# GpSimd operations that carry a dependency on the latest two-operand step of VectorE

## The chip, the cores and the metric

The kernel runs on one core of a Trainium2 chip, as one launch. The metric is the device time of that launch in microseconds (us). Before the change it is 1239.37 us, the median of three runs (1239.02 to 1239.99). The engines are named as in the profile: PE is TensorE's matrix multiply and PEld its weight load, DVE is VectorE, ACT is ScalarE, POOL is GpSimd, SP is SyncE, which issues most of the transfers.

## The reference

The reference is attention over the 32 largest scores of each row, followed by a layer of three products of which the largest is taken, and an output product:

```python
scores = scale * np.matmul(q, k.transpose(0, 1, 3, 2))      # 8 batches, 8 heads, 576 x 576, head dim 64
kth = np.partition(scores, -32, axis=-1)[..., -32:-31]
scores = np.where(scores >= kth, scores, -1e9)
attn = softmax(scores)                                       # sum + 1e-9 in the denominator
x = (attn @ v) as (4608, 512)
h = np.maximum(np.maximum(x @ w1, x @ w2), x @ w3)           # 512 -> 768
out = h @ w_out                                              # 768 -> 512, float32
```

The weights are drawn as float64 numbers, so they reach the chip as pairs of 32-bit words.

## The kernel before

The attention is cut into units. A unit is one or two blocks of 128 query rows for a pair of heads (or the last 64 rows of two pairs), and it has two or four tiles of 128 rows by 576 scores. For each unit TensorE makes the scores (line 465), ScalarE copies them out of the accumulators into tiles `ssb` (473), and VectorE takes the eight largest of each of seven stretches of a row (482). From these small lists a pivot per row is worked out (lines 496 to 514); the last but one of its steps, line 512, is a scalar_tensor_tensor on two SBUF operands. ScalarE writes the sign of pivot minus score into a tile `w` and counts it (522). GpSimd multiplies score and sign, in place in `w` (line 527, the "window product"), VectorE takes the eight largest of the product (531, the MAX8 that follows a window product), and three small steps pick the threshold out of them (542, 545, 547). Then VectorE masks the scores in place (line 570: a scalar_tensor_tensor with two SBUF operands of 576 columns), ScalarE takes the exponential (579), TensorE transposes it (630) and multiplies it with the values (655), and the result is cut into a high and a low half of 16 bits: high by ScalarE (675), low by GpSimd (679).

The weights have to be turned from pairs of words into float32 first. This is the decode: three VectorE steps on 1024 or 512 columns (lines 257, 258, 259), of which the second and the third read two SBUF operands. ScalarE squares each decoded part (268), a scale follows from it (275, 285), ScalarE scales and casts the part (319, 322), and GpSimd subtracts for the low half (325). The scaled part lies in one of two buffers `ws` until GpSimd is done. The MLP's first layer (711) makes three products per block; ScalarE and VectorE take the largest (718, 720); ScalarE makes the high half (723) and GpSimd the low half (726). The second layer is line 771.

So GpSimd has five kinds of work: 288 window products (527), the low halves of the weights (325), of x (679) and of h (726), and eight small additions of a check (612).

The order of all this is not that of the source. Every step is a `Piece` with an engine, an estimated cost, the pieces that it needs, the ring of buffers that it takes and a rank. `in_order` (line 67) goes through the pieces like a clock: it picks the piece that can start earliest by its own estimates, calls its `run`, which writes the instructions, and moves the engine's estimated free time. So the instructions of each engine stand in a fixed order, that in which `run` was called, and they wait for each other by semaphores only as their data requires. Pieces of the MLP go into a list `fill` that TensorE takes from when nothing of the attention is ready.

Some VectorE pieces carry `alone=True`: the decode, the pivot's step 4 (line 512), the first two steps of the pick (542, 545), the mask (570) and a check (607). For these the planner's estimate keeps VectorE and GpSimd apart:

```python
        if x.alone:
            t = max(t, free["POOL"] + LOCK_A)
        elif x.engine == "POOL":
            t = max(t, shut[0] + LOCK_B)
```

Here `shut[0]` is the estimated end of the latest such piece, LOCK_A is -144 ns and LOCK_B is -103 ns. This sets the order and the estimated times only; no instruction waits for it.

Of the kernel before, what the change touches and what calls it, by code (L numbers as in the profile page):

```python
# [14 lines left out]
ALU = mybir.AluOpType  # L15
# [8 lines left out]
NW = 9  # L24
SHRINK = 2.0 ** -61
# [38 lines left out]
        self.size, self.users = size, []  # L64


def in_order(pieces, fill):

    queues, fills = {e: [] for e in LATE}, {e: [] for e in LATE}
    for x in sorted(pieces, key=lambda x: x.rank):
        queues[x.engine].append(x)
    for x in fill:
        fills[x.engine].append(x)
    free = {e: 0.0 for e in LATE}
    mode, shut = [None], [0.0]

    def ready(x):
        t = free[x.engine]  # L80
        for y in x.needs:
            if y.start is None:
                return None
            t = max(t, y.seen(x.engine) + x.slack)
        ahead = {}
        for ring, releases in x.takes:
            k = len(ring.users) - ring.size + ahead.get(ring, 0)
            ahead[ring] = ahead.get(ring, 0) + 1
            for y in ring.users[k] if k >= 0 else ():
                if y.start is None:  # L90
                    return None
                t = max(t, y.seen(x.engine))
        if x.engine == "PE":
            t += SWITCH[mode[0], x.mode]
# [5 lines that stand above are left out]
        return t  # L100

    left = len(pieces) + len(fill)
    while left:
        best = None
        low = min((q[0].rank for q in queues.values() if q), default=0.0)
        for e in LATE:
            some = [x for x in queues[e][:WINDOW] if x.rank <= low + LEAD]
            some = some + fills[e][:1] if e == "PE" else fills[e][:1] + some
            could = [(t, x) for x in some if (t := ready(x)) is not None]
            if could:  # L110
                other = could.pop() if e == "PE" and fills[e][:1] == [could[-1][1]] else None
                if could:
                    first = min(t for t, _ in could) + PATIENCE[e]
                    same = [c for c in could if c[1].mode and c[0] <= first + STICK] if e == "PE" and mode[0] else []
                    t, x = same[0] if same else next(c for c in could if c[0] <= first)
                    wait = STICK if same else SWITCH[mode[0], x.mode] + AHEAD_OF_FILL
                if not could or other and other[0] < t - wait:
                    t, x = other
                if best is None or t < best[0]:
                    best = t, x  # L120
        assert best, [(e, len(q), len(fills[e])) for e, q in queues.items()]
        t, x = best
        (fills if fills[x.engine][:1] == [x] else queues)[x.engine].remove(x)
        x.start = t
        free[x.engine] = t + x.cost
        if x.engine == "PE":
            mode[0] = x.mode
        if x.alone:
            shut[0] = t + x.cost
        for ring, releases in x.takes:  # L130
            ring.users.append(releases)
        x.run()
        left -= 1


# [13 lines left out]
def kernel(ctx, tc, q, k, v, moe_w1, moe_w2, moe_w3, moe_w_out, out):  # L149
    nc = tc.nc  # L150
# [99 lines left out]
    def decode(j, part):  # L250

        at0, n = place(j)
        raw = raw_of[j].rearrange("p c (n t) -> p (c n) t", t=2) if j < 3 * NB else raw_of[j].rearrange("p (n t) -> p n t", t=2)
        m = n // DECODES if j < 3 * NB else n
        low, top = (raw[:, part * m:(part + 1) * m, t] for t in range(2))
        w = wall.bitcast(I32)[:, at0 + part * m:at0 + (part + 1) * m]
        nc.vector.tensor_scalar(w, top, 3, 0x3FFFFFFF, ALU.logical_shift_left, ALU.bitwise_and)
        nc.vector.scalar_tensor_tensor(w, low, 29, w, ALU.logical_shift_right, ALU.bitwise_or)
        nc.vector.scalar_tensor_tensor(w, top, -0x40000000, w, ALU.bitwise_and, ALU.bitwise_or)

    squares_of = {}

# [44 lines left out]
    def cut(j, part):  # L307

        at0, n = place(j)
        m = min(n, 2 * CUT)  # L310
        at0 += part * m
        w = wall[:, at0:at0 + m].rearrange("p (c n) -> p c n", n=CUT)
        hi, lo = (wall.bitcast(F16)[:, 2 * at0:2 * (at0 + m)].rearrange("p (c t n) -> p t c n", t=2, n=CUT)[:, t] for t in range(2))
        box = {}

        def scaled():
            down = scale_of[f"w{j}"][0] if j < 3 * NB else scale_of["rows"][:, (j - 3 * NB) * P // CUT:(j - 3 * NB) * P // CUT + 1]
            box["ws"] = io.tile([P, 2 * CUT], F32, name="ws", bufs=2).rearrange("p (c n) -> p c n", n=CUT)
            nc.scalar.activation(box["ws"], w, AF.Copy, scale=down)

        def high():
            nc.scalar.copy(hi, box["ws"])

        def low():
            nc.gpsimd.tensor_tensor(lo, box["ws"], hi, ALU.subtract)  # L325
        return scaled, high, low

    pieces, fill = [], []
# [161 lines left out]
    def pivot(n, piece):  # L490

        d = st[n]
        nt, L, nA = d["nt"], d["L"], d.get("nA")
        if piece == 1:
            for t in range(nt):
                nc.vector.max(b9s[n % 3][:, t, 1:9], L[:, t, :, 4:8])
        elif piece == 2:
            n8 = d["n8"] = sm.tile([P, 4, 2, 8], F32, name="n8", bufs=NSM)
            for t in range(nt):
                nc.vector.max(n8[:, t, 0], nA[:, t].rearrange("p g j -> p (g j)"))  # L500
            nb = d["nb"] = sm.tile([P, 4], F32, name="nb", bufs=3)
            nc.vector.tensor_reduce(nb[:, :nt], nA[:, :nt, :, 0], AX.X, ALU.min)
        elif piece == 3:
            nR = sm.tile([P, 4, 4 * G], F32, name="nR", bufs=1)
            for t in range(nt):
                nc.vector.match_replace(nR[:, t], d["n8"][:, t, 0], nA[:, t].rearrange("p g j -> p (g j)"), -BIG)  # L506
            for t in range(nt):
                nc.vector.max(d["n8"][:, t, 1], nR[:, t])
        elif piece == 4:
            z = d["z"] = sm.tile([P, 4, 9], F32, name="z", bufs=2)  # L510
            low = d["n8"].rearrange("p t a b -> p t (a b)")[:, :nt, 4 * G - 24:4 * G - 15]
            nc.vector.scalar_tensor_tensor(z[:, :nt], low, -SHRINK, b9s[n % 3][:, :nt], ALU.mult, ALU.min)
        else:
            nc.vector.tensor_reduce(d["Q"][:, :, 0:1], d["z"][:, :nt], AX.X, ALU.max)  # L514

# [8 lines left out]
    def window(n, t):  # L524

        d = st[n]
        nc.gpsimd.tensor_tensor(d["w"][t], d["ssb"][t], d["w"][t], ALU.mult)  # L527

    def below(n, t):
        d = st[n]  # L530
# [2 lines left out]
    def pick(n, step):  # L533


        d = st[n]
        nt = d["nt"]
        if step == 0:
            d["oh"] = sm.tile([P, 4, NW], F32, name="oh", bufs=2)
        best = d["oh"]  # L540
        if step == 0:
            nc.vector.scalar_tensor_tensor(best[:, :nt], spots.unsqueeze(1).to_broadcast((P, nt, NW)), 1.0,
                                           d["cnt"][:, :nt].unsqueeze(2).to_broadcast((P, nt, NW)), ALU.mult, ALU.is_gt)
        elif step == 1:
            nc.vector.tensor_tensor(best[:, :nt], best[:, :nt], d["Q"], ALU.mult)
        else:
            nc.vector.tensor_reduce(d["kth"], best[:, :nt], AX.X, ALU.max)

# [17 lines left out]
    def mask(n, t):  # L566

        d = st[n]
        ss = d["ssb"][t]
        nc.vector.scalar_tensor_tensor(ss, ss, d["kth"][:, t:t + 1], ss, ALU.is_lt, ALU.subtract,  # L570
                                       accum_out=d["lost"][:, t:t + 1])

    def expo(n, t):
# [83 lines left out]
    def x_at(n, t):  # L657
        b, hps, us = units[n]
        if us[0] < NU:
            return t[:, hps[0], us[0] * P:(us[-1] + 1) * P]  # L660
        return t[:, hps[0]:hps[0] + 2, MAIN:S]
# [14 lines left out]

    def low_x(n):
        xh, xl = x_of[units[n][0]]
        nc.gpsimd.tensor_tensor(x_at(n, xl), xs_of(n), x_at(n, xh), ALU.subtract)  # L679
        st.pop(n)  # L680

    H, so_of = [], {}
    WIDE = S - 2 * P
# [2 lines left out]
    def mlp(b, first, spans, tiles, alone, needs, rank):  # L686
# [36 lines left out]
            nc.scalar.copy(H[0][:, f, cs], box["h"][:, :w])  # L723

        def low_h(f, cs, w, box):
            nc.gpsimd.tensor_tensor(H[1][:, f, cs], box["h"][:, :w], H[0][:, f, cs], ALU.subtract)  # L726

        for c0, c1 in spans:
            w = c1 - c0
# [258 lines left out]
    for b in range(B):  # L988
# [4 lines left out]
            fill.extend(every)  # L993
        x_done[b].append(last)

    with tc.manual_schedule():
        in_order(pieces, fill)


    limits = const.tile([P, 2], F32, name="limits")  # L1000
# [95 lines left out]
```

## Time and profile before

| | |
|---|---|
| median of three runs | 1239.37 us |
| profiled execution | 1238.17 us |
| its span, first to last instruction | 1236.4 us |
| PE busy | 1142.7 us, 8817 instructions |
| DVE busy | 1120.1 us, 5413 instructions |
| ACT busy | 1032.7 us, 2692 instructions |
| POOL busy | 570.5 us, 503 instructions |

The profile is one execution of the program. "Busy" is the time in which an engine had at least one instruction running; an instruction that is held by something inside the engine still counts as busy, so a held instruction shows as a longer one and not as idle time. Semaphore instructions don't count as busy. In the rows, `out<-in` gives the program's tiles, then the shape, then how often.

### The profile page before, as it was taken

The numbers are of one execution on the slowest core, as the hardware profiler recorded it, in microseconds if no ns is written. First come the engines' busy times: TensorE is split into PE (matmuls) and PEld (weight loads), VectorE is DVE, ScalarE is ACT, GpSimd is POOL, SyncE is SP. The second block draws the span as 40 slices with busy tenths as digits, with TensorE's granted clock in tenths as the row PEclk, the third lists the DMA queues.
The fourth block names the chain that finished last, engine by engine and source line by source line (L and its number), as shares of the span: only waits on it lengthen the run. The fifth ranks groups of instructions, "written<-read, shape, count | busy, mean of one in ns | idle before, by whom it ended". The sixth has DMA issues, their size and how long they took to land.

```text
span 1236.4 us, 27297 instructions
## 1 busy us (share of the span) xinstructions
PE 1142.7 (92%) x8817; PEld 778.5 (63%) x8817; DVE 1120.1 (91%) x5413; ACT 1032.7 (84%) x2692; POOL 570.5 (46%) x503
## 2 busy tenths in 40 slices
PE   5357877999899999999999999999999999999998
PEld 2124653566586766766676667666676767766765
DVE  7999998999999999999899999999899999999311
ACT  6588887999989898998889998998889989888421
POOL 2453654545445445355354554454553544546111
PEclk7576986999899999999999999999999999999999
DMA  6241220202010202011110102020101100000000
GB/s 240 71 141 52 63 82 11 88 2 69 18 54 18 61 1 86 2 48 31 49 31 27 52 10 78 3 72 6 49 31 48 31 25 23 10 10 1 18 18 29
DMA packets 25750, 54.38 MB, mean 44 GB/s; under 512 B 2688, under 2 KB 2944, under 8 KB 25600
## 3 DMA queue, kind: packets, MB, share of 16 engines
q1 hardware_dynamic: 25296, 52.14, 12.9%
q8 instruction: 71, 1.16, 0.4%
q14 instruction: 79, 0.65, 0.2%
q10 hardware_dynamic: 304, 0.43, 0.1%
HBM read 43.12 MB, written 9.44 MB: 43 GB/s over the span
## 4 chain that ended last, share of the span: by engine, by line
PE 37%; DVE 23%; ACT 7%; POOL 2%; issue 2%; DVEq 0%; ACTq 0%
PE m L711 17%; DVE L L482 6%; DVE ssb L570 5%; PE m L771 5%; PE tr L655 5%; PE s L465 4%; PE tr L630 4%; DVE Q L531 4%; ACT pm L579 2%; POOL w L527 2%; DVE h L720 2%; ACT w L522 1%; ACT pT L638 1%; DVE nR L506 1%; PE tr L627 1%
## 5 line engine op out<-in xcount | busy, mean ns | idle before, releaser
L527 POOL TENSOR_TENSOR w<-ssb,w 128x576 f32<-128x576 f32 x288 | 410.9, 1451 | 288.5 <-ACT w L522 287.3
L711 PE MATMUL m<-xh,wall 128*128 128x256 f16 (+1 forms) x2304 | 433.9, 286 | 3.1 <-DVE h L720 3.1
L711 PEld LDWEIGHTS <-wall 128*128 128x128 f16 x3456 | 337.7, 98 | 87.8 <-issue 12.3
L711 PE MATMUL m<-xl,wall 128*128 128x320 f16 (+1 forms) x1152 | 329.4, 286 | 0.1
L482 DVE MAX8 L<-ssb 128x8 f32<-128x82 f32 (+1 forms) x2016 | 312.0, 229 | 5.6 <-ACT ssb L473 5.6
L579 ACT ACTIVATE pm<-ssb,nb 128x576 f32<-128x576 f32 x288 | 223.3, 776 | 55.8 <-DVE ssb L570 55.2
L570 DVE SCALAR_TENSOR_TENSOR ssb<-ssb,kth 128x576 f32<-128x576 f32 x288 | 235.8, 851 | 2.4
L522 ACT ACTIVATE w<-ssb,Q 128x576 f32<-128x576 f32 x288 | 223.3, 776 | 6.3 <-DVE Q L514 6.1
L638 ACT COPY pT<-tr 128x512 f32<-128x512 f32 (+1 forms) x432 | 216.6, 514 | 12.2 <-PE tr L627 6.5
L531 DVE MAX8 Q<-w 128x8 f32<-128x576 f32 x288 | 213.7, 750 | 13.6 <-POOL w L527 12.6
L465 PE MATMUL s<-qk 64*128 64x288 f32 (+1 forms) x1280 | 195.3, 455 | 14.4 <-ACT ssb L473 9.2
L630 PE MATMUL tr<-ident,pm 128*128 128x128 f32 x1152 | 180.2, 282 | 25.5 <-ACT pm L579 12.6
L473 ACT ACTIVATE ssb<-s 128x576 f32<-128x576 f32 x288 | 185.0, 654 | 12.5 <-PE s L465 12.5
L655 PE MATMUL tr<-pT,vt 128*64 128x256 f32 (+1 forms) x1920 | 187.5, 347 | 2.3 <-ACT pT L638 2.3
L630 PEld LDWEIGHTS tr<-ident,pm 128*128 128x128 f32 x1152 | 131.2, 143 | 78.9 <-ACT pm L579 22.8
L655 PEld LDWEIGHTS tr<-pT,vt 128*64 128x64 f32 x1920 | 112.7, 144 | 74.5 <-issue 19.5
L465 PEld LDWEIGHTS s<-qk 64*128 64x128 f32 (+1 forms) x1280 | 100.9, 186 | 81.2 <-ACT ssb L473 30.5
L720 DVE SCALAR_TENSOR_TENSOR h<-m,rises,h 128x256 f32<-128x256 f32 (+1 forms) x192 | 97.3, 507 | 52.4 <-PE m L711 51.7
L726 POOL TENSOR_TENSOR hl<-h,hh 128x256 f16<-128x256 f32 (+1 forms) x96 | 72.9, 759 | 151.1 <-ACT hh L723 151.0
L771 PE MATMUL m<-wall,hh 128*128 128x512 f16 (+1 forms) x444 | 130.6, 376 | 0.9 <-POOL wall L325 0.9
L679 POOL TENSOR_TENSOR xl<-xs,xh 128x256 f16<-128x256 f32 (+1 forms) x80 | 56.0, 700 | 133.7 <-ACT xh L675 128.6
L771 PE MATMUL m<-wall,hl 128*128 128x512 f16 (+1 forms) x222 | 83.4, 376 | 0.0
(95 smaller groups left out, 1107.2 us busy)
## 6 DMA issues: line engine op xcount, KB each, us to landing
vt<-in_v_dram SPq DMA_DIRECT2D x32, 320.0 KB, 3.2
qk<-in_k_dram SPq DMA_DIRECT2D x34, 288.0 KB, 3.1
qk<-in_q_dram SPq DMA_DIRECT2D x33, 288.0 KB, 3.7
wall<-in_moe_w_dram SPq DMA_DIRECT2D x16, 512.0 KB, 4.7
out_dram<-ob SPq DMA_DIRECT2D x32, 256.0 KB, 2.0
wall<-in_moe_w_out_dram SPq DMA_DIRECT2D x3, 512.0 KB, 3.8
ssb<-in_moe_w_out_dram SPq DMA_DIRECT2D x3, 512.0 KB, 3.5
wall<-in_moe_w_dram SPq DMA_DIRECT2D x4, 256.0 KB, 6.0
```

Source lines behind the costliest of these rows:

```text
L465: nc.tensor.matmul(to[:, h, :HALF], both[sl, 0, c0:c0 + m], both[sl, 1, i * HALF:(i + 1) * HALF], start=True, stop=True)
L482: nc.vector.max(d["L"][:, t, k, :], d["ssb"][t][:, EDGES[k]:EDGES[k + 1]])
L522: nc.scalar.activation(d["w"][t], d["ssb"][t], AF.Sign, bias=d["Q"][:, t, 0:1], scale=-1.0, accum_out=d["cnt"][:, t:t + 1])
L527: nc.gpsimd.tensor_tensor(d["w"][t], d["ssb"][t], d["w"][t], ALU.mult)
L531: nc.vector.max(d["Q"][:, t, 1:NW], d["w"].pop(t))
L570: nc.vector.scalar_tensor_tensor(ss, ss, d["kth"][:, t:t + 1], ss, ALU.is_lt, ALU.subtract, accum_out=d["lost"][:, t:t + 1])
L579: nc.scalar.activation(d["pm", t // 2][:, t % 2], d["ssb"][t], AF.Exp, bias=d["nb"][:, t:t + 1], scale=-1.0 / SHRINK, accum_out=d["sums"][ ...
L630: nc.tensor.transpose(pt[:, j * P:(j + 1) * P], pm[:, i, 64 * i + j * P:64 * i + (j + 1) * P], ident)
L638: nc.scalar.copy(pT[:, 512 * i:512 * i + m] if i < 2 else pT[:, 8 * P:10 * P], pt[:, :m])
L655: nc.tensor.matmul(to, vt[:, block if i < 4 else 8 + h, :], keys, start=(i == 0), stop=(i == 4))
L711: nc.tensor.matmul(box["ps", i][:, :c1 - c0], a, bb[:, kc, c0:c1], start=(kc == 0 and k == 0), stop=(kc == KC - 1 and k == 2))
L771: nc.tensor.matmul(box["po"][:n, :ds.stop - ds.start], a[:, f, cs], columns_of(bb, ds), start=(f == 0 and k == 0), stop=(f == FC - 1 and k ...
```

## The change

`x.run()` now hands back the instruction that it wrote, for the pieces concerned. `in_order` remembers the latest one from a piece with `alone` set, and for each GpSimd piece that hands one back it calls `behind`, which records a dependency with a semaphore: the GpSimd instruction is to wait until that VectorE instruction is done. The check's step (607) and its addition on GpSimd (612) hand nothing back and stay as they are. In the decode it is the third step (259) that is handed back. Where an instruction has a wait of its own already, a further one becomes a semaphore instruction ahead of it on the same engine.

```diff
-def in_order(pieces, fill):
+def in_order(pieces, fill, behind):
...
-    mode, shut = [None], [0.0]
+    mode, shut, two = [None], [0.0], [None]
...
-        x.run()
+        made = x.run()
+        if x.alone and made is not None:
+            two[0] = made
+        elif x.engine == "POOL" and made is not None and two[0] is not None:
+            behind(made, two[0])
         left -= 1
...
-        nc.vector.scalar_tensor_tensor(w, top, -0x40000000, w, ALU.bitwise_and, ALU.bitwise_or)
+        return nc.vector.scalar_tensor_tensor(w, top, -0x40000000, w, ALU.bitwise_and, ALU.bitwise_or)
...
-            nc.gpsimd.tensor_tensor(lo, box["ws"], hi, ALU.subtract)
+            return nc.gpsimd.tensor_tensor(lo, box["ws"], hi, ALU.subtract)
...
+    def behind(later, earlier):
+
+        tc.add_manual_dep(later.ins, earlier.ins.name, mybir.DependencyInfo(mybir.DependencyClass.Sync, mybir.DependencyReason.DATA))
+
     with tc.manual_schedule():
-        in_order(pieces, fill)
+        in_order(pieces, fill, behind)
```

The same `return` is added to lines 512, 527, 542, 545, 570, 679 and 726. Nothing else changes: the pieces, their estimates and so the order of each engine's instructions are the same.

## Rows read from the trace of the kernel before

**Rows 1.** The page: busy us, share of the span, instructions of each engine.
```profile
PE 1142.7 (92%) x8817; PEld 778.5 (63%) x8817; DVE 1120.1 (91%) x5413; ACT 1032.7 (84%) x2692; POOL 570.5 (46%) x503
```

**Rows 2.** Stages: length, then PE, PEld, DVE, ACT, POOL busy; PEclk; DMA; GB/s.
```profile
0.00:100.00 100.00, 50.11 (x232) 25.92 (x234) 91.78 (x389) 67.91 (x148) 43.85 (x34) 0.69 0.41 140
100.00:200.00 100.00, 77.87 (x550) 53.80 (x550) 95.61 (x359) 82.01 (x211) 50.53 (x41) 0.81 0.18 61
...
400.00:500.00 100.00, 99.72 (x820) 69.75 (x818) 97.28 (x488) 90.30 (x244) 50.21 (x46) 1.00 0.15 46
```

**Rows 3.** The chain of waits, near its end: start us, us, what.
```profile
1163.58 18.34 PE m L711 x168
```

**Rows 4.** Groups of VectorE by form, 30 to 200 us: busy us, mean ns, idle before.
```profile
L570 DVE SCALAR_TENSOR_TENSOR ssb<-ssb,kth 128x576 f32<-128x576 f32 x30 | 28.8, 980 | 0.2
...
L259 DVE SCALAR_TENSOR_TENSOR wall<-wall 128x1024 int32<-128x1024 int32 x9 | 15.2, 1689 | 0.3
L258 DVE SCALAR_TENSOR_TENSOR wall<-wall 128x1024 int32<-128x1024 int32 x9 | 14.0, 1560 | 0.3
...
L259 DVE SCALAR_TENSOR_TENSOR wall<-wall 128x512 int32<-128x512 int32 x3 | 3.5, 1171 | 0.1
L258 DVE SCALAR_TENSOR_TENSOR wall<-wall 128x512 int32<-128x512 int32 x3 | 3.2, 1055 | 0.1
...
L545 DVE TENSOR_TENSOR oh<-oh,Q 128x18 f32<-128x18 f32 x2 | 1.6, 791 | 0.0
```

**Rows 5.** Single lines over the whole run: min/median/max ns, first and last start, forms.
```profile
L570 DVE SCALAR_TENSOR_TENSOR ssb<-ssb,kth x288: 789/815/2025, 22.2 to 1146.2; 128x576 f32<-128x576 f32 x144
...
L258 DVE SCALAR_TENSOR_TENSOR wall<-wall x12: 693/1226/2308, 42.9 to 183.9; 128x1024 int32<-128x1024 int32 x9, 128x512 int32<-128x512 int32 x3
L258 DVE SCALAR_TENSOR_TENSOR wall<-ssb,wall x3: 693/693/693, 174.2 to 189.1; 128x512 int32<-128x512 int32 x3
...
L545 DVE TENSOR_TENSOR oh<-oh,Q x80: 160/195/1414, 21.7 to 1145.0; 128x36 f32<-128x36 f32 x64, 128x18 f32<-128x18 f32 x16
```

**Rows 6.** Timeline of VectorE, from 42 us: start us, us, what.
```profile
42.85 2.31 DVE L258 SCALAR_TENSOR_TENSOR wall<-wall 128x1024 int32<-128x1024 int32 x1
45.19 2.30 DVE L259 SCALAR_TENSOR_TENSOR wall<-wall 128x1024 int32<-128x1024 int32 x1
...
49.25 0.74 DVE L531 MAX8 Q<-w 128x8 f32<-128x576 f32 x1
```

**Rows 7.** Timeline of GpSimd, from 29 us; in brackets idle before and its releaser.
```profile
29.55 4.13 POOL L527 TENSOR_TENSOR w<-ssb,w 128x576 f32<-128x576 f32 x3
40.86 7.89 POOL L527 TENSOR_TENSOR w<-ssb,w 128x576 f32<-128x576 f32 x4 [7.18 <-ACT w L522]
```

**Rows 8.** Groups of VectorE by form, 200 to 400 us.
```profile
L570 DVE SCALAR_TENSOR_TENSOR ssb<-ssb,kth 128x576 f32<-128x576 f32 x53 | 42.5, 842 | 0.5
```

**Rows 9.** Line 527 over the whole run; POOLq is GpSimd's sequencer.
```profile
L527 POOL TENSOR_TENSOR w<-ssb,w x288: 1395/1412/2382, 15.3 to 1138.9; 128x576 f32<-128x576 f32 x144
L527 POOLq EVENT_SEMAPHORE  x34: 17/17/17, 29.4 to 1091.9; - x34
```

**Rows 10.** Timeline of ScalarE, at 47 us.
```profile
47.58 1.06 ACT L268 ACTIVATE junk<-wall 128x1024 bf16<-128x1024 f32 x1 [4.52 <-DVE wall L259]
```

**Rows 11.** Timeline of VectorE, at 560 and at 1093 us.
```profile
560.89 0.83 DVE L570 SCALAR_TENSOR_TENSOR ssb<-ssb,kth 128x576 f32<-128x576 f32 x1
...
1093.71 0.20 DVE L512 SCALAR_TENSOR_TENSOR z<-n,b 128x36 f32<-128x36 f32 x1
...
1095.27 0.76 DVE L531 MAX8 Q<-w 128x8 f32<-128x576 f32 x1
```

**Rows 12.** Waits over the whole run: us in total, times, longest us.
```profile
DVE Q L531 <- POOL w L527: 12.6, 22, 1.4
...
DVE xs L672 <- PE tr L655: 7.0, 5, 1.9
```

**Rows 13.** Timeline of GpSimd, at 560 us.
```profile
559.70 3.30 POOL L527 TENSOR_TENSOR w<-ssb,w 128x576 f32<-128x576 f32 x2
```

More of the change, by code (lines that the diff above doesn't have):

```diff
@@ L511, in pivot @@
             low = d["n8"].rearrange("p t a b -> p t (a b)")[:, :nt, 4 * G - 24:4 * G - 15]
-            nc.vector.scalar_tensor_tensor(z[:, :nt], low, -SHRINK, b9s[n % 3][:, :nt], ALU.mult, ALU.min)
+            return nc.vector.scalar_tensor_tensor(z[:, :nt], low, -SHRINK, b9s[n % 3][:, :nt], ALU.mult, ALU.min)
         else:
@@ L526, in window @@
         d = st[n]
-        nc.gpsimd.tensor_tensor(d["w"][t], d["ssb"][t], d["w"][t], ALU.mult)
+        return nc.gpsimd.tensor_tensor(d["w"][t], d["ssb"][t], d["w"][t], ALU.mult)
     def below(n, t):
@@ L541, in pick @@
         if step == 0:
-            nc.vector.scalar_tensor_tensor(best[:, :nt], spots.unsqueeze(1).to_broadcast((P, nt, NW)), 1.0,
+            return nc.vector.scalar_tensor_tensor(best[:, :nt], spots.unsqueeze(1).to_broadcast((P, nt, NW)), 1.0,
                                            d["cnt"][:, :nt].unsqueeze(2).to_broadcast((P, nt, NW)), ALU.mult, ALU.is_gt)
         elif step == 1:
-            nc.vector.tensor_tensor(best[:, :nt], best[:, :nt], d["Q"], ALU.mult)
+            return nc.vector.tensor_tensor(best[:, :nt], best[:, :nt], d["Q"], ALU.mult)
         else:
@@ L569, in mask @@
         ss = d["ssb"][t]
-        nc.vector.scalar_tensor_tensor(ss, ss, d["kth"][:, t:t + 1], ss, ALU.is_lt, ALU.subtract,
+        return nc.vector.scalar_tensor_tensor(ss, ss, d["kth"][:, t:t + 1], ss, ALU.is_lt, ALU.subtract,
                                        accum_out=d["lost"][:, t:t + 1])
@@ L678, in low_x @@
         xh, xl = x_of[units[n][0]]
-        nc.gpsimd.tensor_tensor(x_at(n, xl), xs_of(n), x_at(n, xh), ALU.subtract)
+        made = nc.gpsimd.tensor_tensor(x_at(n, xl), xs_of(n), x_at(n, xh), ALU.subtract)
         st.pop(n)
+        return made
     H, so_of = [], {}
@@ L725, in low_h @@
         def low_h(f, cs, w, box):
-            nc.gpsimd.tensor_tensor(H[1][:, f, cs], box["h"][:, :w], H[0][:, f, cs], ALU.subtract)
+            return nc.gpsimd.tensor_tensor(H[1][:, f, cs], box["h"][:, :w], H[0][:, f, cs], ALU.subtract)
         for c0, c1 in spans:
```

## The prediction

> **What bounds the kernel now.** I read the busy shares first, then the stages, then the chain of waits, then VectorE's and GpSimd's groups, then the timelines of both at the places that stood out. The shares put TensorE and VectorE side by side at about 92%, with GpSimd at less than half [rows 1]. That average hides two stages, and the stage table separates them [rows 2]. In the first 100 us TensorE is busy for 50.11 us and in the second for 77.87 us, while VectorE is busy for 91.78 and 95.61: here VectorE decodes the weights beside the attention work, and TensorE waits for it through ScalarE. From 400 us on TensorE is busy for 99.72 us of each 100, and at the very end the chain is TensorE's MLP products alone [rows 3]. So VectorE sets the pace up to roughly 200 us, all engines are near full to 400 us, and then TensorE sets it. Since each engine's order is fixed, whatever makes the state of 200 us come earlier moves all that follows by about as much; time that VectorE saves after 400 us is worth little.
>
> In VectorE's own stage I looked for instructions that take longer than their work. The window's groups [rows 4] against the same forms' usual durations [rows 5] show it: the steps that read two SBUF operands are stretched, while the rest are not. The timeline shows with whom. The decode's second step takes 2.31 us at 42.85 us and the third 2.30 us at 45.19 us [rows 6], against 1.226 us usually; in just that time GpSimd has four window products that take 7.89 us, where three took 4.13 us at 29.55 us [rows 7]. Each engine waits for the other to finish a whole instruction, alternately.
>
> **What the change removes.** Each GpSimd operation is to wait for the last two-operand step that the planner placed ahead of it. I worked through the order of creation in the planner and set each of the 488 operations concerned beside the step in the trace. 90 of them started before that step had ended; those are the ones that move. In 30 to 200 us, the excess of the stretched steps over the usual duration is: mask 30 x (980 - 815) ns = 4.95 us; decode of 1024 columns, third step 9 x (1689 - 1226) = 4.17 us, second step 9 x (1560 - 1226) = 3.01 us; decode of 512 columns 3 x (1171 - 693) = 1.43 us and 3 x (1055 - 693) = 1.09 us; second step of the pick on two tiles 2 x (791 - 160) = 1.26 us [rows 4, 5]. The sum is 15.9 us. For nearly all of it, the GpSimd operation that held VectorE up stands behind the step in the planner's order, and only began first because VectorE was later than planned. Under the change it begins afterwards, so I take the whole 15.9 us as removed from VectorE's queue; the bounds are 0 (if the collisions only move elsewhere; less than 0 is excluded here, since the steps themselves wait for nothing new) and 17 (with the small steps that I left out). From 200 to 400 us the masks give another 53 x (842 - 815) = 1.4 us [rows 5, 8]; as TensorE is nearly full there I count 1.0.
>
> **What it adds.** First, an extra semaphore instruction on GpSimd where the step is a new one: 155 of the 488. Those that exist take 17 ns each [rows 9], so 2.6 us in all on an engine with 54% idle; taken at 0, and 2.6 us if nothing hid it. Second, the wait itself. A semaphore from VectorE reaches another engine in about 0.09 us: the third decode step ends at 45.19 + 2.30 = 47.49 us and ScalarE's square that waits for it begins at 47.58 us [rows 6, 10]. A window product needs 1.41 us [rows 9], so it is done 1.50 us after the step's end. Behind a waiting GpSimd operation the next window products, low halves of weights, of x and of h queue up. Those who wait for them are VectorE's MAX8 over the window, ScalarE through the two buffers of scaled weights, and TensorE's products.
>
> The window products are the only ones close to VectorE. 29 of the 288 would be held. The MAX8 that reads a product comes behind the step on VectorE, so the question is whether 1.50 us of other work lies between. At the first collision the step ends at 47.49 us and the second product's MAX8 begins at 49.25 us [rows 6], which is 1.76 us later; the room is above 1.50 us in 25 of the 29. The tightest is at 1093.71 us: the step ends 0.20 us later, the MAX8 begins at 1095.27 us, room 1.36 us [rows 11], which costs about 0.15 us. VectorE waits for window products for 12.6 us in all today [rows 12], so these few tenths stay small. For the stage up to 200 us I allow 0.5 us for them and 0.5 us for ScalarE, where the low halves of weights hold their two buffers longer.
>
> Where the step begins first, GpSimd's operation is held already today, and the wait only takes the start-up from it that it does while held. At 559.70 us two products take 3.30 us [rows 13]; the second began some 1.38 us after the first, ran into the mask that ends at 561.72 us [rows 11], and ended at 563.00 us, 1.28 us after it. Under the change it ends 0.09 + 1.41 = 1.50 us after it: 0.22 us later.
>
> **How much arrives.** 15.9 + 1.0 - 1.0 = 15.9 us earlier on VectorE. Not all of it passes: VectorE then meets more often the results of TensorE and ScalarE, which have their own durations there (TensorE's granted clock is 0.69 and 0.81 of full speed, a mix of its two levels, 1.2 and 2.4 GHz [rows 2]); today it waits 7.0 us for the value products [rows 12]. I take off 2.5 us for this, by that row: a third of the waits again. What is left is 13.4 us. After 400 us VectorE loses some of its stalls too, and the GpSimd results come some 0.22 us later; both are beside a full TensorE, and I count them as zero together. The profiled execution took 1238.17 us (its span of 1236.4 and 1.8 around it), so it would become 1224.8; the median of the runs is 1.2 us above it, so the forecast for the median is **1226 us**.
>
> **Rivals.** *The state moves less.* ScalarE, or the chain of squares, scales and cuts of the weights, takes over as the bound in the first 200 us, and VectorE's 15.9 us come back as waits. For it: ScalarE is at 82.01 us of 100 in the second stretch, and TensorE is slow there [rows 2]. Against it: VectorE has hardly any idle time there, and ScalarE's own wait of 4.52 us at the first collision is for VectorE [rows 10]. It would give 1233 to 1240, at the end no change at 1239. That the waits are already implied by the data (a window product follows a sign, which follows an earlier step) belongs here too, and the 90 early starts speak against it.
>
> *GpSimd's queue becomes the brake, and it is slower.* An operation that waits for a late step holds the window products behind it, VectorE's MAX8 starves, and the step that others wait for comes later still. The place is the stage from 400 us on, where VectorE is at 97.28 us of 100 and has no slack. The price is the 0.22 us above for each product that is held: at all 29, without cover, 6.4 us, and 1246 us if nothing of the ramp arrives; 1242 to 1246 in all. It decides when the room falls below 1.50 us, which it does at 4 of the 29. The Trainium skill (SBUF — State Buffer, section "Who interferes with whom") says that the port pair shared by VectorE and GpSimd belongs to whichever instruction starts first until that ends, so by this rule a wait shortens nothing for the two together: the stall changes sides, and 15.9 us move onto GpSimd's queue. The trace agrees that whole instructions are held (2.31 us against 1.226 us [rows 5, 6]).
>
> *More arrives.* All 17 us and the 1.4 us pass on, and the ramp's TensorE runs at a higher granted clock because it idles less: 1217 to 1220.
>
> **How the numbers follow.** The forecast has 0.64 (1220 to 1233), more 0.08, less or nothing 0.16, slower 0.12. The range reaches from 1217, which takes in the larger gain, to 1240, which takes in the unchanged time; what is left out is mainly the slower case. About 0.2%, 2.5 us, is what a measurement of this kernel can tell from no change. Of the case with less, 0.06 is still faster by over that; so faster 0.78, same 0.10, slower 0.12.
>
> **What would show it.** In the profile after, the decode's second and third steps of 1024 columns should take 1.23 us each time, the masks' mean in 30 to 200 us should fall to about 820 ns, and the group of window products should come near 1.41 us mean, with waits of GpSimd for the mask or the decode in the list of waits. TensorE's busy time in the first 200 us should rise by some 10 us while the stretch from 400 us on stays at over 99%. VectorE's wait for the window products should stay below 15 us. The prediction is wrong if the stretched steps go but the tail of MLP products starts no earlier than 1157 us instead of 1163.58 [rows 3]; then the gain was given back as waits. It is wrong in its first step if the stretched durations stay.

## The result and the profile after

The changed kernel takes 1223.38 us, the median of four runs (1222.68 to 1224.47), against 1239.19 us (1238.48 to 1239.99) beside it: ratio 0.9873, 95% interval 0.9856 to 0.9890, a gain of 15.8 us. A second set of five runs gave 1223.57 us against 1239.70 us, ratio 0.9873 (0.9855 to 0.9891). The profiled execution took 1222.68 us, its span 1220.9 us, the mean granted clock of TensorE 0.959. The lines of the new file stand four or five below those of before.

The page's busy shares after, to be read against [rows 1]:

```profile
PE 1137.3 (93%) x8817; PEld 776.7 (64%) x8817; DVE 1104.6 (90%) x5413; ACT 1031.5 (84%) x2692; POOL 545.9 (45%) x503
```

VectorE and GpSimd have become less busy by 15.5 and 24.6 us with the same instructions. That is held time: it had counted as busy.

The stages after, with the columns of [rows 2]:

```profile
0.00:100.00 100.00, 50.15 (x244) 26.45 (x244) 91.70 (x428) 75.34 (x167) 41.56 (x40) 0.71 0.41 140
100.00:200.00 100.00, 84.15 (x619) 57.64 (x620) 94.86 (x397) 87.08 (x221) 45.80 (x44) 0.84 0.19 64
...
400.00:500.00 100.00, 99.35 (x797) 70.76 (x796) 97.24 (x490) 91.52 (x246) 48.83 (x45) 1.00 0.12 37
```

VectorE is as busy in the first 200 us as before (186.6 against 187.4), but it starts 825 instructions there instead of 748, and TensorE is busy for 134.3 us instead of 128.0. From 400 to 500 us TensorE is full in both kernels. The chain of waits ends as before, and the MLP's tail of [rows 3] starts 15.52 us earlier:

```profile
1148.06 18.34 PE m L716 x168
```

VectorE's groups by form, 30 to 185 us (nearly the work of 30 to 200 us of before: the same decode steps, 28 masks instead of 30), against [rows 4]; busy us, mean ns, idle before:

```profile
L574 DVE SCALAR_TENSOR_TENSOR ssb<-ssb,kth 128x576 f32<-128x576 f32 x28 | 23.9, 874 | 0.2
L262 DVE SCALAR_TENSOR_TENSOR wall<-wall 128x1024 int32<-128x1024 int32 x9 | 11.0, 1226 | 0.3
L263 DVE SCALAR_TENSOR_TENSOR wall<-wall 128x1024 int32<-128x1024 int32 x9 | 11.0, 1226 | 0.3
...
L262 DVE SCALAR_TENSOR_TENSOR wall<-wall 128x512 int32<-128x512 int32 x3 | 2.1, 693 | 0.1
L263 DVE SCALAR_TENSOR_TENSOR wall<-wall 128x512 int32<-128x512 int32 x3 | 2.1, 692 | 0.1
...
L549 DVE TENSOR_TENSOR oh<-oh,Q 128x18 f32<-128x18 f32 x2 | 0.8, 425 | 0.0
```

The decode's second and third steps are free of stalls. The masks are not: 874 ns, against 980 before and 815 at the median of the whole run. Nor is the second step of the pick on two tiles: 425 ns, against 791 before and 160 at best. The first collision, in the timelines of VectorE and of GpSimd, against [rows 6, 7]:

```profile
42.79 1.23 DVE L262 SCALAR_TENSOR_TENSOR wall<-wall 128x1024 int32<-128x1024 int32 x1
44.05 1.22 DVE L263 SCALAR_TENSOR_TENSOR wall<-wall 128x1024 int32<-128x1024 int32 x1
45.19 0.75 DVE L535 MAX8 Q<-w 128x8 f32<-128x576 f32 x1
45.86 1.25 DVE L486 MAX8 L<-ssb 128x8 f32<-128x82 f32 x8
47.03 0.74 DVE L535 MAX8 Q<-w 128x8 f32<-128x576 f32 x1
```
```profile
40.80 1.41 POOL L531 TENSOR_TENSOR w<-ssb,w 128x576 f32<-128x576 f32 x1 [7.17 <-ACT w L526]
45.42 4.12 POOL L531 TENSOR_TENSOR w<-ssb,w 128x576 f32<-128x576 f32 x3 [3.22 <-DVE wall L263]
```

One product runs ahead of the decode, and three wait until its third step is done. They begin 0.15 us after that step's end (44.05 + 1.22 = 45.27), and the first MAX8 that reads one of them comes at 47.03 us, 0.2 us after the product's end: VectorE loses nothing. Where the two engines held each other up in turn there is now one wait of 3.22 us, on an engine that is idle for more than half the time.

The list of waits after (us in total, times, longest us), for the window products and who reads them, against [rows 12]:

```profile
POOL w L531 <- DVE ssb L574: 15.9, 14, 2.8
DVE Q L535 <- POOL w L531: 13.0, 23, 1.4
...
POOL w L531 <- DVE wall L263: 10.3, 4, 3.3
...
DVE xs L676 <- PE tr L659: 6.6, 6, 1.5
```

VectorE's own waits are as they were: 13.0 against 12.6 us for GpSimd, 6.6 against 7.0 us for TensorE.

### The profile page after: what moved, and what is told of

Same layout as the page of the kernel before. It is cut to its first block, busy times and chain, and to the rows that moved or that the text cites. A ratio compares the mean times of both kernels' runs of the same rounds, so it can differ in the third digit from the quotient of the medians.

```text
span 1220.9 us, 27377 instructions
## 1 busy us (share of the span) xinstructions
PE 1137.3 (93%) x8817; PEld 776.7 (64%) x8817; DVE 1104.6 (90%) x5413; ACT 1031.5 (84%) x2692; POOL 545.9 (45%) x503
## 4 chain that ended last, share of the span: by engine, by line
PE 44%; DVE 36%; ACT 13%; POOL 4%; issue 3%; DMA 0%; POOLq 0%; ACTq 0%; DVEq 0%
PE m L716 18%; DVE L L486 8%; DVE ssb L574 8%; PE tr L659 8%; PE s L469 6%; PE m L776 6%; DVE Q L535 6%; PE tr L634 5%; POOL w L531 4%; ACT w L526 3%; ACT pm L583 3%; DVE h L725 3%; ACT pT L642 2%; DVE nR L510 2%; ACT ssb L477 1%
## 5 line engine op out<-in xcount | busy, mean ns | idle before, releaser
L531 POOL TENSOR_TENSOR w<-ssb,w 128x576 f32<-128x576 f32 x288 | 400.1, 1412 | 289.1 <-ACT w L526 259.5
L574 DVE SCALAR_TENSOR_TENSOR ssb<-ssb,kth 128x576 f32<-128x576 f32 x288 | 230.3, 832 | 2.4
L469 PE MATMUL s<-qk 64*128 64x288 f32 (+1 forms) x1280 | 191.6, 449 | 13.8 <-ACT ssb L477 8.8
L477 ACT ACTIVATE ssb<-s 128x576 f32<-128x576 f32 x288 | 184.9, 654 | 12.6 <-PE s L469 12.5
L731 POOL TENSOR_TENSOR hl<-h,hh 128x256 f16<-128x256 f32 (+1 forms) x96 | 70.4, 733 | 159.4 <-ACT hh L728 80.0
L683 POOL TENSOR_TENSOR xl<-xs,xh 128x256 f16<-128x256 f32 (+1 forms) x80 | 50.0, 625 | 141.2 <-ACT xh L679 41.7
```

The lines of the kernel that those rows point to most:

```text
L469: nc.tensor.matmul(to[:, h, :HALF], both[sl, 0, c0:c0 + m], both[sl, 1, i * HALF:(i + 1) * HALF], start=True, stop=True)
L531: return nc.gpsimd.tensor_tensor(d["w"][t], d["ssb"][t], d["w"][t], ALU.mult)
L574: return nc.vector.scalar_tensor_tensor(ss, ss, d["kth"][:, t:t + 1], ss, ALU.is_lt, ALU.subtract, accum_out=d["lost"][:, t:t + 1])
```

## The experiments

The order of each engine's instructions is the same in all these kernels; only waits differ. So one and the same instruction can be found in two traces, and "shift" below is the difference of its start to the kernel before. The changed kernel's is -8.3 us for what stood at 100 us on VectorE, -14.0 at 200, -15.3 at 400, -14.9 at 600 and -15.5 at the end. In sum the gain is made in the first 400 us, nearly all of it in the first 200. A second trace of the same kernel has -13.6 at 200 us, -12.7 at 250, -14.6 at 400 and -14.7 at the end, so up to 400 us a shift can be off by about 1 us. In the two kernels that give no dependency after 400 us (ramp only, and up to 400 us) it stays within 0.2 us from there to the end.

**Only the ramp, and only what follows.** The dependency is given until the last part of the weights is decoded (about 185 us), or only after that.

```diff
+    decodes = 0
...
-            two[0] = made
+            decodes += x.alone and x.cost in (DECODE_IN, DECODE_OUT)
+            two[0] = made if decodes < 15 or x.alone and x.cost in (DECODE_IN, DECODE_OUT) else None    # ramp
+            two[0] = made if decodes == 15 and not (x.alone and x.cost in (DECODE_IN, DECODE_OUT)) else None    # late
```

> The dependency is given only until the last of the 15 decode parts is written (some 36 of the 90 operations that were held). Theory (VectorE sets the pace up to about 200 us, so only the stalls taken from it there count; the changed kernel's VectorE is 14.0 us ahead at 200 us): nearly the whole gain, 1223 to 1227 us. Rival (each held operation is worth the same wherever it lies, 36 of 90): 1239.2 - 0.4 x 15.8 = about 1233 us.

> The dependency is given only after the last decode part. Theory: TensorE is full there, so no change but the rest between 190 and 400 us: 1236 to 1240 us. Rival (54 of 90 held operations): about 1230 us. A second rival (the waits after the ramp cost GpSimd and VectorE something): above 1240 us.

Measured: the ramp alone 1226.54 us, ratio 0.9903 (0.9887 to 0.9919), a gain of 12.1 us; the rest alone 1237.18 us, 0.9989 (0.9978 to 1.0000), 1.4 us. The ramp's shift is -13.0 us at 200 and then -11.5 to -11.0 to the end. Both lie in the ranges of the theory. So the stage named in the prediction carries most of the gain, most of what it earns arrives, and the waits of the rest, given alone, earn little, at most 2.7 us by the interval.

**Where the last 3 us come from.** The ramp alone lacks some 3.7 us of the whole. This kernel gives the dependency up to 400 us of the planner's clock.

```diff
-            two[0] = made
+            two[0] = made if t < 400e3 else None
```

> The dependency is given while the planner's own clock is below 400 us, so in the ramp and in the stage in which all engines are nearly full, and not after. Theory (the kernel with the dependency in the ramp alone was 13.0 us ahead at 200 us and 11.1 at 340, the changed kernel 14.0 and 15.6: the rest of the gain is kept between 200 and 400 us, and nothing comes after): 1222 to 1225 us, as the changed kernel. Rival (the waits after 400 us bring the missing 2 to 3 us): 1226 to 1228 us.

Measured: 1222.33 us against 1239.02, ratio 0.9864 (0.9848 to 0.9881), which can't be told from the whole change. So the stretch of 200 to 400 us gives the remainder, the waits after 400 us together bring and cost nothing that can be measured (each kind by itself does, see below), and three quarters of the added semaphore instructions can go: GpSimd has 91 here, 150 with the whole change, 70 before.

**Which steps are waited for.** GpSimd waits for the latest decode part only, or for all the other two-operand steps only.

```diff
-            two[0] = made
+            if x.alone and x.cost in (DECODE_IN, DECODE_OUT):          # decode
+                two[0] = made
...
-            two[0] = made
+            if not (x.alone and x.cost in (DECODE_IN, DECODE_OUT)):    # no decode
+                two[0] = made
```

> GpSimd waits for the latest decode part alone, not for masks, pivots or picks. Theory (a sum over VectorE's stalls): the decode's part of the sum, 4.17 + 3.01 + 1.43 + 1.09 = 9.7 us: 1229 to 1231 us, with the decode steps at 1.23 us and the masks still stretched. Rival (what counts is that the weights are ready earlier, the masks' stalls are hidden): 1223 to 1226 us.

> The complement: GpSimd waits for the latest mask, pivot or pick step, not for the decode. Theory: masks 4.95 + pick 1.26 = 6.2 us: 1232 to 1235 us, and with the decode-only kernel the two gains add up to about that of the change. Rival (weights): 1237 to 1240 us.

Measured: decode only 1227.82 us, 0.9916 (0.9898 to 0.9934), 10.8 us; the others only 1231.03 us, 0.9940 (0.9925 to 0.9956), 7.6 us. Both came out some 1 us faster than the ranges expected. The trace of the first is of its slowest run (1232.13 us), so only durations are read from it. VectorE's groups, 30 to 185 us, first with the decode only, then without it (lines are one higher than after):

```profile
L575 DVE SCALAR_TENSOR_TENSOR ssb<-ssb,kth 128x576 f32<-128x576 f32 x26 | 24.6, 969 | 0.2
L264 DVE SCALAR_TENSOR_TENSOR wall<-wall 128x1024 int32<-128x1024 int32 x9 | 11.1, 1228 | 0.3
L263 DVE SCALAR_TENSOR_TENSOR wall<-wall 128x1024 int32<-128x1024 int32 x9 | 11.0, 1225 | 0.3
```
```profile
L575 DVE SCALAR_TENSOR_TENSOR ssb<-ssb,kth 128x576 f32<-128x576 f32 x26 | 22.2, 878 | 0.2
L264 DVE SCALAR_TENSOR_TENSOR wall<-wall 128x1024 int32<-128x1024 int32 x9 | 14.1, 1571 | 0.3
L263 DVE SCALAR_TENSOR_TENSOR wall<-wall 128x1024 int32<-128x1024 int32 x9 | 14.0, 1559 | 0.3
```

The stalls come apart cleanly: the first kernel frees the decode and leaves the masks (969 ns against 980 before), the second frees the masks as far as the whole change does (878 against 874) and leaves the decode. The gains add up to 18.4 us, against the whole's 15.8, but each of the three is uncertain by about 2 us, so the excess is not clear of noise. The two halves need not add up: an operation whose latest step is left out waits for an earlier one instead.

**Which GpSimd operations wait.** Only the window products, or only the low halves.

```diff
-        elif x.engine == "POOL" and made is not None and two[0] is not None:
+        elif x.engine == "POOL" and x.cost == 1373 and made is not None and two[0] is not None:   # window products
+        elif x.engine == "POOL" and x.cost != 1373 and made is not None and two[0] is not None:   # low halves
```

> Only the 288 window products carry the dependency; the low halves of weights, x and h don't. Theory (what counts is who held VectorE up in the ramp: about half of the removed stalls there, 8.1 us, lie beside window products): 1230 to 1233 us. Rival (only the window products feed VectorE, so only they matter): 1223 to 1226 us.

> The complement: the 200 low halves carry the dependency, the window products don't. Theory: the other half of the removed stalls, 8.2 us: 1230 to 1233 us, and with the window products' kernel the two gains add up to that of the change. Rival: 1237 to 1240 us.

Measured: window products 1234.14 us, 0.9959 (0.9947 to 0.9972), 5.6 us; low halves 1228.77 us, 0.9912 (0.9896 to 0.9928), 10.9 us. The sum, 16.5 us, is close to the gain of 16.1 us on the same chip, but the parts are not equal, as I had expected: the first lies above its range and the second below. The traces show where they part, and most of it is not in the ramp. At 200 us the two kernels are ahead by nearly the same, 6.4 us with the window products and 5.8 with the low halves. Then the lead of the window products shrinks, to 4.9 us at 400 us and 2.4 at the end, and that of the low halves grows, to 7.6 and 9.8. The MLP's tail, first with the window products, then with the low halves, against 1163.58 before [rows 3]:

```profile
1161.20 18.34 PE m L716 x168
```
```profile
1153.81 18.34 PE m L716 x168
```

(The first trace is of one of that kernel's slower runs, 1236.09 us: its tail comes 2.4 us earlier, where the median gains 5.6, and its lead at 200 us may be larger in a usual run.) After 400 us, then, the waits of the window products alone cost 2.5 us and those of the low halves alone bring 2.1, though TensorE is nearly full there. One of the steps that the low halves no longer hold up there, before and with the low halves:

```profile
498.87 1.17 DVE L570 SCALAR_TENSOR_TENSOR ssb<-ssb,kth 128x576 f32<-128x576 f32 x1
```
```profile
491.49 0.82 DVE L574 SCALAR_TENSOR_TENSOR ssb<-ssb,kth 128x576 f32<-128x576 f32 x1
```

The whole change has both kinds, and there they cancel: its shift is -15.3 us at 400 us and -15.5 at the end. How the window products' waits come to cost 2.5 us was not taken apart. A kernel with all waits up to 400 us and those of the low halves alone after it was not run.

**The wait on the other side.** The same pairs are kept apart by making VectorE's two-operand step wait for the latest GpSimd operation ahead of it; GpSimd waits for no step.

```diff
-        if x.alone and made is not None:
+        if x.engine == "POOL" and made is not None:
             two[0] = made
-        elif x.engine == "POOL" and made is not None and two[0] is not None:
+        elif x.alone and made is not None and two[0] is not None:
             behind(made, two[0])
```

> The reverse dependency alone: each two-operand step of VectorE waits for the latest GpSimd operation that the planner placed ahead of it, and GpSimd waits for none. Theory (it matters who waits; VectorE's stalls behind operations that overtook stay, and in 35 places VectorE now waits a little longer, 1.3 us in the ramp and up to 6 us after it): 1239 to 1244 us. Rival (keeping the two apart is what helps, on whichever side): below 1232 us.

Measured: 1250.29 us, 1.0091 (1.0074 to 1.0109), slower by 10.6 us, beyond the range expected. The shift is +2.4 us at 200 us, +2.3 at 400 and grows to +12.3 at the end, mostly in steps of about 1.3 us. One such step, in the timelines of VectorE and of GpSimd (in brackets idle before and its releaser):

```profile
532.23 1.37 DVE L546 SCALAR_TENSOR_TENSOR oh<-spots,cnt 128x18 f32<-128x18 f32 x1 [1.23 <-POOL w L531]
```
```profile
530.79 5.51 POOL L531 TENSOR_TENSOR w<-ssb,w 128x576 f32<-128x576 f32 x4
```

And the same step in the kernel before, where it is line 542:

```profile
528.10 1.32 DVE L542 SCALAR_TENSOR_TENSOR oh<-spots,cnt 128x18 f32<-128x18 f32 x1
```

Before, the step was held once, for most of 1.32 us. Now VectorE waits 1.23 us for a product. Four products stand in a row without a gap, 5.51 us in all, so the second of them begins at about 532.17 us, 0.06 us ahead of the step, and holds it for 1.37 us again. The stall is paid twice. TensorE, nearly full in this stage, then waits for a mask's exponential, where it had no such wait before, and the delay goes to the end:

```profile
540.99 0.66 PE L634 MATMUL tr<-ident,pm 128*128 128x128 f32 x4 [0.73 <-ACT pm L583]
```

**Every step of VectorE.** GpSimd waits for the latest VectorE step of any kind ahead of it.

```diff
-        if x.alone and made is not None:
-            two[0] = made
+        if x.engine == "DVE":
+            two[0] = newest()    # the instruction written last
...
```

> A stricter wait: each GpSimd operation waits for the latest VectorE step of any kind ahead of it in the order, with 437 semaphore instructions on GpSimd instead of 150. Theory (a wait is free only where the MAX8 that reads the product comes over 1.5 us after the step's end): in the trace of the kernel before, 435 of 488 operations would be held, and 162 of the window products have less room, short by 72 us in all, 52 of them after 400 us, where a delay of VectorE is passed on: much slower, 1260 to 1300 us. Rival (GpSimd is idle for more than half of the time, so holding it costs nothing): 1222 to 1230 us.

Measured: 1316.42 us, 1.0622 (1.0605 to 1.0640), slower by 77.4 us and above the range. Its list of waits:

```profile
POOL w L531 <- DVE L L486: 184.9, 64, 14.3
DVE Q L535 <- POOL w L531: 88.1, 134, 1.6
```

and its stage from 400 us:

```profile
400.00:500.00 100.00, 91.52 (x708) 57.92 (x705) 90.69 (x467) 83.70 (x223) 41.80 (x38) 1.00 0.11 37
```

GpSimd now waits for the MAX8s of line 486, which were not held up (218 to 248 ns before), so a product can end some 1.5 us after a step that stands right ahead of its reader, and VectorE waits for products 134 times instead of 23. The shift is -5.8 us at 200 us, then grows by some 8 to 10 us per 100 us. This is the brake of the second rival, and it shows that the gain hangs on which steps are waited for.

## Why the prediction was right

The forecast was 1226 us, a gain of 13.4 us; 15.8 were measured. The mechanism held in the stage that was named: the decode's stalls went, the state at 200 us came earlier by what VectorE had lost, and it arrived at the end. The nearness of the number is in part luck. The removed stalls were put 2.4 us too high, and 2.5 us were taken off for waits that did not come; the two errors cancel.

*The removed stalls: 15.9 us taken, 13.5 measured (12.3 in the second trace of the changed kernel).* I set each VectorE instruction of the first 200 us beside itself in the two traces and added the differences of duration: -13.5 us, of which the decode lines give -8.3. The decode's second and third steps came out at 1226 ns as said. What failed is "I take the whole 15.9 us as removed": the dependency holds back only GpSimd operations that stand behind the step in the order. One that stands ahead of it and is still running holds VectorE up as before. After, in VectorE's and GpSimd's timelines:

```profile
156.12 1.21 DVE L574 SCALAR_TENSOR_TENSOR ssb<-ssb,kth 128x576 f32<-128x576 f32 x1
```
```profile
155.31 1.41 POOL L531 TENSOR_TENSOR w<-ssb,w 128x576 f32<-128x576 f32 x1 [0.80 <-DVE ssb L574]
```

The product had waited for the mask before this one, began 0.81 us ahead of this one and held it up for 0.4 us. That is why the masks' mean is 874 ns and not the 820 that I named. Part of the stalls also moved to the decode's first step, which reads one SBUF operand and which I had not counted: its 15 instructions take 1.4 us more than before. So the reading that the steps with two SBUF operands are stretched "while the rest are not" was wrong, and the trace before showed it (last section).

*What comes back as waits: 2.5 us taken, none measured.* VectorE was to wait for TensorE's and ScalarE's results a third more. It did not: 6.6 us against 7.0 [rows 12], and the shift at 200 us, -14.0, is slightly more than the -13.5 of the durations. The row on which I based this term was of the right wait but gave no reason for its growth: the value products depend on VectorE's masks themselves, so they could come earlier with them.

*200 to 400 us: 1.0 taken.* The durations there fell by 1.0 us, as said; the shift grew by 1.3 (from -14.0 to -15.3). In the second trace these are 1.6 and 1.0. The kernel with the dependency up to 400 us, 16.7 us gained against the ramp's 12.1, puts the worth of this stretch at some 4 us, on two different chips. The traces say where most of that lies. The ramp-only kernel falls back from -13.0 us at 200 to -11.1 at 400; 1.0 us of it goes at one MAX8 that waits for a window product. The changed kernel frees three steps between 274 and 301 us that the ramp-only kernel leaves held: a pivot's step (678 to 195 ns) and two masks (1340 to 817 and 1443 to 819 ns); 0.4 us of this comes back at a pivot's step that is held in their place. Why the ramp-only kernel falls back at all stays open; given alone, the waits after the ramp earned 1.4 us.

*The added cost: 1.0 us taken.* It is not to be seen in the first 200 us. The semaphore instructions on GpSimd went from 70 to 150, so 80 came and not 155. VectorE's wait for products went from 12.6 to 13.0 us, below the 15 named. The window products' mean is 1412 ns, as said, against 1451 before; their semaphores are 51 and take 17 ns at the median. One size was off: the hand-over from VectorE to GpSimd takes 0.15 us and not the 0.09 read from ScalarE [rows 6, 10], so a product ends 1.56 us after the step; the room was still enough.

*TensorE.* Busy time in the first 200 us rose by 6.3 us, not by 10; in the second trace by 4.0. The products begun there say more: 863 (860 in the second trace) instead of 782. That a higher granted clock of TensorE made the gain, which is part of the rival "more arrives", does not fit the traces: the clock in the first and second 100 us was 0.69 and 0.81 before, 0.71 and 0.84 after, and 0.68 and 0.90 in the second trace, with nearly the same shift at 200 us; the reversed kernel had 0.68 and 0.84 and was behind.

*After 400 us, net zero.* The sum holds, as the kernel that stops there shows. The reason given, that both terms are beside a full TensorE, does not: the waits of the low halves alone gain 2.1 us after 400 us and those of the window products alone lose 2.5. Both pass on, and they cancel; I had not worked that out.

*The rivals.* "The state moves less" fell with the shift of -14.0 at 200 us. "GpSimd's queue becomes the brake" has a small price at these steps, the 2.5 us of the window products after 400 us, which the low halves pay back, and a large one when all steps are waited for. The stall did change sides, to an engine that was idle for 54% of the time, where little of it is felt: VectorE's busy time is 15.5 us less, and its own waits hardly grew. "More arrives", 1217 to 1220, lies 3 us below what was measured.

## What to carry to other kernels

When two engines hold each other up instruction by instruction, look in the groups by form for means above the same form's minimum, and put the wait on the engine with idle time, for those steps of the other alone that are actually held; a wait on the busy engine can cost twice, when the idle engine's next queued operation slips in during the hand-over. Count as removed only the stalls whose culprit stands behind the held step in the order. Don't count a stage as neutral because another engine is nearly full in it: here savings and delays of about 2 us each passed on from such a stage, and only their sum was zero.

## What was not expected of the hardware

The decode's first step is a tensor_scalar with a single SBUF operand, and it is stretched beside GpSimd all the same. So is a small tensor_scalar on 128x3. The single lines of both before (min/median/max ns):

```profile
L257 DVE TENSOR_SCALAR wall<-ssb x3: 416/427/952, 173.8 to 188.1; 128x512 int32<-128x512 int32 x3
```
```profile
L295 DVE TENSOR_SCALAR rises<-backs,down_wi x3: 230/956/1291, 65.3 to 130.3; 128x3 f32<-128x3 f32 x3
```

The first of them after, and its longest case in both timelines:

```profile
L261 DVE TENSOR_SCALAR wall<-ssb x3: 419/428/1247, 162.3 to 174.2; 128x512 int32<-128x512 int32 x3
```
```profile
174.19 1.25 DVE L261 TENSOR_SCALAR wall<-ssb 128x512 int32<-128x512 int32 x1
```
```profile
173.74 1.41 POOL L531 TENSOR_TENSOR w<-ssb,w 128x576 f32<-128x576 f32 x1 [1.88 <-DVE wall L263]
```

The product ends at 175.15 us and the step at 175.44, 0.29 us later: of a step that takes 0.43 us at the median, 0.29 us lay behind the product's end. The Trainium skill (SBUF — State Buffer, section "Who interferes with whom") counts tensor_scalar among the instructions that can take the shared pair and so meet GpSimd; the trace agrees, with 1247 ns against 428.

The other surprise is the nearly full stage. From 400 to 600 us TensorE is busy for 99.5% of the time before the change, yet what VectorE and GpSimd gain or lose after 400 us is not hidden there: 2.1 us gained with the low halves, 2.5 lost with the window products, and 10.0 lost in the reversed kernel, whose shift goes from +2.3 to +12.3.
